# Two attention branches in one Trainium2 program: half tiles for A's values, a second query tile turned by TensorE, and a new order of work

## The chip, the cores and the metric

The program runs on one core of a Trainium2 chip. The core has five engines with a queue of instructions each: TensorE (PE in the profile, with its weight loads PEld), VectorE (DVE), ScalarE (ACT), GpSimd (POOL) and SyncE (SP), which here only issues transfers. The metric is the device time of the program in microseconds (us), as the median of several executions.

## The reference

Two independent branches work on 2048 tokens of width 640, with 32 heads of 20 channels, and their outputs stand side by side. The core of each, cut:

```python
# A: four segments of 512 tokens, causal attention inside a segment, and a memory over the earlier ones
p = _softmax(einsum('bhqd,bhkd->bhqk', qs, ks) * scale + mask)
a_dot = einsum('bhqk,bhkd->bhqd', p, vs)
a_mem = einsum('bhld,bhde->bhle', phi(qs), M) / (einsum('bhld,bhd->bhl', phi(qs), z)[..., None] + 1e-06)
o = g * a_mem + (1.0 - g) * a_dot
M = M + einsum('bhld,bhle->bhde', phi(ks), vs); z = z + einsum('bhld->bhd', phi(ks))
...
return o @ wo
# B: causal attention with a sliding window of 256 tokens
scores = where(mask, einsum('bhqd,bhkd->bhqk', q, k) * Dh ** (-0.5), -1e9)
o = einsum('bhqk,bhkd->bhqd', _softmax(scores), v)
return o.reshape(B, S, D) @ wo
```

## The kernel before

The work is cut into eight chunks of 512 tokens, A and B in turn: A0, B0, A1, B1, A2, B2, A3, B3 (numbers 0 to 7). A chunk needs its projections (q, k, v), its scores, the exponentials, the masks, the product with the values, the division, the memory (A only) and the output projection.

**Scores and values.** `score_batch` (line 801) issues one batch: matmuls of 20 channels for four heads at a time, on four row strips of the array, into two PSUM tiles named `sc`, and behind them two exponentials on ScalarE (line 830) that write probability tiles `pt`. There are 153 batches and three `sc` tiles, so a batch's second tile waits until the exponential of the batch before has read it. GpSimd zeroes triangles of `pt` (line 869), VectorE multiplies others with a mask (line 847). `av` (line 883) and, in the last chunk, `av_tile` (line 904) multiply `pt` with the values, on four column strips. VectorE turns the result in 32x32 blocks (line 949), takes reciprocals (line 977), and GpSimd multiplies into `o` (line 987).

**Projections.** `wide` (line 935, or line 930 on four column strips) issues the matmuls of 512 or 320 columns for q, k, v and the output, into one of two PSUM banks, `m0` and `m1`, from which VectorE copies them (lines 557, 733, 738, 1100). A bank is free again when that copy is done.

**Values of A.** `vA` is one tile of 128 x 4 x 696 for all 32 heads. `v_job` writes it in two jobs, heads 0 to 15 and 16 to 31 (line 733). After each job two transfers copy half of its rows into `vS` (line 757), from where the products with the squares on the diagonal read. The program waits by tile: an instruction that reads one half of `vA` can wait for a write to the other half.

**The end.** A query tile of the last chunk (128 tokens) needs `o` with its channels on the partitions. For tiles 0, 1 and 2 `final` stores `o` to a buffer in memory (line 1021, four transfers), and a transposing transfer brings it back (line 1040); `final_job` then multiplies with the output weights. The last tile is turned on TensorE in `last_job`: four matmuls with a unit matrix (line 1122) and sixteen small ones (line 1134) put `o` into PSUM, VectorE and ScalarE copy it (lines 1126 and 1140) into free corners of `pq` and `pkT`, ten matmuls with re-ordered output weights follow in two halves (`last_half`), ScalarE copies the one (line 1157) and VectorE the other (line 1160), and two transfers store them (line 1164).

**The order.** No scheduler runs at run time. `PLAN` lists every step of TensorE: `S` or `s` is a score batch, `A` the product with the values for the next group of heads, `M` a product with the memory, `k20*5` five matmuls of the k projection of chunk 2, `o71*4` four of the output projection of chunk 7's tile 1, `d4` the memory's update, `z0` a step of `last_job`. Where an `A` follows a capital `S`, the projections beside it run on column strips. The instructions of the other engines are placed as a model of their times in `Flow` says when TensorE gets there; at run time each engine takes its queue in that order.

Of the kernel before, what the change touches and what calls it, by code (L numbers as in the profile page):

```python
# [60 lines left out]
PLAN = (  # L61
# [22 lines left out]

# [183 lines left out]
class _K:  # L268
# [391 lines left out]
    def dm_job(self, seg, pkT, v):  # L660
# [12 lines left out]
        for some in (own, [(lambda kt, h=h: spare[:, kt, R2 * h:R2 * h + R2], R2,  # L673
# [6 lines left out]
            for lhs, rows, xs, g0 in some:  # L680

                gs = [g0] if g0 is not None else sorted(MEM2[x][1] for x in xs)
                n = W * len(gs)
                v0 = at_head(4 * gs[0])
                for kt in range(LT):
                    nc.tensor.matmul(dM[0:rows, at:at + n], lhsT=lhs(kt),  # L686
                                     rhs=v[:, kt, v0:v0 + n],
                                     start=(kt == 0), stop=(kt == LT - 1))
                f.on_pe("full", 4 * mm_ns(n), 4 * n, 0.0, 4)
                at += n  # L690
                if (rows, xs) != (some[-1][1], some[-1][2]):
                    yield 0.0
# [22 lines left out]
    def v_job(self, n, half, w_ap, v, gate, needs):  # L715
# [5 lines left out]
        for tt in range(LT):  # L721
            yield "bank"
            ps, bi = self.bank()
            for kt in range(self.KT):
# [4 lines left out]
            src = ps[:, 0:320].rearrange("p (h e) -> p h e", e=DH)  # L729
            dst = v[:, tt, HV * half:HV * half + 16 * VS].rearrange(  # L730
                "p (h e) -> p h e", e=VS)[:, :, 0:DH]
# [15 lines left out]
    def v_squares(self, n, half, v):  # L747


        f = self.f  # L750
        s = slice(HV * half, HV * half + HV)
        tok = v[0:SH, :, s].rearrange("p (a b) c -> p a b c", b=2)
        t = f.dve + 138.0

        def go():
            for odd in (0, 1):
                self.nc.sync.dma_start(
                    out=self.vS[SH * odd:SH * odd + SH, odd * 2:odd * 2 + 2, s],
                    in_=tok[:, :, odd, :])
                tl = f.on_dma(1, 410.0, t) + (1200.0 if n == 0 else 0.0)  # L760
            for g in range(4 * half, 4 * half + 4):
                self.mark(tl, n, "v", g)
        f.at(t, go)

    def v_ends(self, n, c, half, v):
# [15 lines left out]
        def go():  # L781
# [3 lines left out]
            for g in range(4 * half, 4 * half + 4):  # L785
                self.mark(tl, n, "v", g)
        f.at(t, go)

    def v_tile(self, name, now=True):
# [84 lines left out]
    def av(self, parts, g, vof):  # L874
# [4 lines left out]
        for n_, (ref, q0, nq, c0, pts) in enumerate(parts):  # L879
            v = vof(ref)  # L880
            for j in range(4):
                h = 4 * g + j
                nc.tensor.matmul(O[HD * j:HD * j + HD, q0:q0 + nq],  # L883
                                 lhsT=v[:, at_head(h):at_head(h) + HD],
                                 rhs=pts[j // 2][:, j % 2, c0:c0 + nq],
# [162 lines left out]
    def final_job(self, n, wo, out2d, r0, col, t0, t1, there):  # L1048
# [4 lines left out]
        for tt in range(t0, t1):  # L1053
            if n == len(self.chunks) - 1 and tt == LT - 2:

                row = r0 + tt * P
                for hf in range(2):
                    yield "bank"
                    self.last_half(hf, lambda m: oT[:, m, tt * P:(tt + 1) * P], wo,
                                   out2d[row:row + P], col)  # L1060
                continue
            while self.ring("ot", NOT) is None:
# [45 lines left out]

    def last_job(self, o, wo, out2d, r0, col, t):


        nc, f = self.nc, self.f
        yield t
        yield self.sc_free[-NSC]
        two = self.ps.tile([P, 2, 512], F32, name="sc", bufs=NSC)
        self.sc_free.append(f.pe + 3000.0)
        own = len(self.sc_free) - 1
        b0 = LT * (LT - 1)
        wide = two[:, 0, :].rearrange("p (j b t) -> p b j t", j=4, b=LT)
        one = self.one[:].rearrange("p (j t) -> p j t", j=4)  # L1120
        for b in range(LT):
            nc.tensor.matmul(wide[:, b], lhsT=o[:, b0 + b, 0:P], rhs=one, start=True, stop=True,
                             skip_group_check=True)
            f.on_pe("full", mm_ns(P), P)
        oT = [self.pq[:, 0, 0:4 * P], self.pkT[:, 0, 0:P]]
        nc.vector.tensor_copy(out=oT[0], in_=two[:, 0, :])
# [16 lines left out]
        oT = [oT[m // 4][:, P * (m % 4):][:, 0:P] for m in range(self.KT)]  # L1143
        row = r0 + (LT - 1) * P
        for hf in range(2):
# [158 lines left out]
    def body(self, xA, A_wq, A_wk, A_wv, A_wo, A_beta, xB, B_wqkv, B_wo, out2d):  # L1304
# [41 lines left out]
        self.vX = big.tile([P, VW], BF16, name="vX")  # L1346
        self.vA = self.v_tile("vA")
        self.vS = big.tile([P, LT, VW], BF16, name="vS")
        self.consts_mz()
# [7 lines left out]
        self.consts_ends()  # L1357
        nc.gpsimd.memset(self.vS[:].bitcast(F32), 0.0)
        f.on_pool(10500.0)
# [208 lines left out]
    def one_group(self, n, kind, c, g, what, parts, left, o_t, groups_done, scro, wo, out2d):  # L1568
# [3 lines left out]
        def vof(ref):  # L1572
            what, u = ref
            if what == "a":
                return self.vA[:, u, :]
            if what in "st":
                return self.vS[:, 2 * (u % 2) + u // 2, :]
            if what == "l":
# [12 lines left out]
        if what == "tile":  # L1591
# [11 lines left out]
            def last(t):  # L1603
                if g0 == G - 4:
                    if qt == LT - 1:
                        self.fins.insert(0, self.job(self.last_job(o, wo["end"], out2d, c * L, col, t), "z0"))
                        return
# [105 lines left out]
```

## Time and profile before

| | us |
|---|---|
| median of three runs | 330.22 |
| lowest and highest | 328.9, 330.69 |
| the profiled execution's own time | 329.68 |
| its span, first to last instruction | 328.0 |
| TensorE busy | 315.8 (96%) |
| ScalarE busy | 299.5 (91%) |
| GpSimd busy | 265.3 (81%) |
| VectorE busy | 255.6 (78%) |

A matmul's busy time overlaps the next one's, so 96% says that TensorE rarely stood idle, not that it worked at its peak. The granted clock of TensorE was 1.00 in all stretches from 0 to 328 us. The views used are the page, the busy time by stretches, the waits (who waited for whom), the chain that ended last, the timeline, and the view of one source line. "Idle before" is the time that an engine had nothing to do before an instruction, and what ended it. What only a comparison of the two built programs shows, the order of instructions on each engine, is not in a profile; such counts are named as counts of the order.

### The profile page before, as it was taken

The page shows a single profiled execution, that of the slowest core. Times are in us where ns is not written, and L with a number is a line of the kernel's source. Part 1 is how long each engine was busy: PE and PEld are TensorE (multiplying, and loading weights), DVE is VectorE, ACT ScalarE, POOL GpSimd, SP SyncE. Part 2 cuts the span into 40 slices and gives each one's busy share as a digit, 9 for nine tenths or more (in the row PEclk, how much of TensorE's full clock was granted, in tenths as well). Part 3 has the DMA queues.
Part 4 walks back from the last instruction along what each step waited for, and adds up shares of the span by engine and source line. Part 5 has one row for each costly group of instructions (what it writes and reads, how often), then busy time and mean ns, then how long its engine had stood idle before and what let it go on. Part 6 is the DMA issues. An engine that isn't in the chain of part 4 may idle for free. (4 is left out here: it accounts for less than half of the span.)

```text
span 328.0 us, 16968 instructions
## 1 busy us (share of the span) xinstructions
PE 315.8 (96%) x7195; PEld 176.3 (54%) x7195; DVE 255.6 (78%) x533; ACT 299.5 (91%) x333; POOL 265.3 (81%) x672
## 2 busy tenths in 40 slices
PE   8999999999999999999999999999999999999995
PEld 2454546555544455555654545456655445666663
DVE  6777767789877887998877897988776788876763
ACT  2979999999999998989999999899999999979982
POOL 8466689998769899977885999998976899998761
PEclk9999999999999999999999999999999999999999
DMA  7975845773689566164689146116968126587752
GB/s 207 400 253 124 199 142 90 162 199 64 137 222 182 108 161 180 38 138 145 142 218 170 28 87 156 52 26 133 156 184 194 26 48 157 141 203 186 119 122 88
DMA packets 76266, 47.45 MB, mean 145 GB/s; under 512 B 48382, under 2 KB 73182, under 8 KB 76190
## 3 DMA queue, kind: packets, MB, share of 16 engines
q1 hardware_dynamic: 75469, 45.71, 58.5%
q8 instruction: 56, 0.92, 1.2%
q10 hardware_dynamic: 720, 0.66, 0.7%
q14 instruction: 21, 0.16, 0.2%
HBM read 17.62 MB, written 16.96 MB: 105 GB/s over the span
## 5 line engine op out<-in xcount | busy, mean ns | idle before, releaser
L830 ACT ACTIVATE pt<-sc 128x1024 bf16<-128x1024 f32 (+2 forms) x306 | 282.5, 1024 | 14.4 <-PE sc L814 12.4
L869 POOL TENSOR_SCALAR_AFFINE_SELECT pt<-pt 128x128 bf16<-128x128 bf16 (+1 forms) x512 | 178.0, 376 | 48.9 <-ACT pt L830 42.0
L949 DVE STREAM_TRANSPOSE tt<-m 128x512 f32<-128x512 f32 x88 | 61.2, 709 | 24.9 <-PE m L883 16.1
L987 POOL TENSOR_TENSOR o<-tt,rr 128x320 bf16<-128x320 f32 x64 | 48.4, 757 | 3.6 <-DVE rr L977 2.6
L814 PE MATMUL sc<-qB,kB 20*64 20x64 bf16 (+2 forms) x1728 | 39.6, 217 | 1.0 <-ACT pt L830 0.3
L935 PEld LDWEIGHTS <-xT 128*128 128x128 bf16 x296 | 26.7, 97 | 18.3 <-issue 6.5
L847 DVE TENSOR_TENSOR pt<-pt,ends 128x1024 bf16<-128x1024 bf16 (+2 forms) x50 | 36.3, 737 | 0.0
L1100 DVE CAST ot<-m 128x320 bf16<-128x320 f32 x58 | 28.1, 486 | 9.4 <-PE m L935 8.2
L814 PEld LDWEIGHTS <-kB 20*64 20x64 bf16 (+1 forms) x1728 | 22.0, 98 | 22.5 <-issue 20.7
L814 PE MATMUL sc<-qA,kA 20*64 20x64 bf16 (+4 forms) x1024 | 33.4, 237 | 0.3 <-ACT pt L830 0.3
L935 PEld LDWEIGHTS <-oT 128*128 128x128 bf16 x244 | 21.4, 97 | 11.9 <-issue 2.6
L814 PEld LDWEIGHTS <-kA 20*128 20x128 bf16 (+1 forms) x1024 | 13.5, 97 | 22.2 <-issue 21.1
L935 PE MATMUL m<-wBv,xT 128*128 128x320 bf16 x147 | 24.2, 299 | 0.9 <-DVE tt L949 0.4
L883 PE MATMUL m<-pt,vA 128*32 128x192 bf16 (+3 forms) x512 | 23.6, 274 | 0.2
L935 PE MATMUL m<-xT,wBq 128*128 128x512 bf16 x82 | 21.4, 380 | 0.3 <-DVE tt L949 0.3
L935 PE MATMUL m<-wo_A,oT 128*128 128x320 bf16 x125 | 21.0, 301 | 0.3 <-DVE kA L557 0.3
L935 PE MATMUL m<-xT,wBk 128*128 128x512 bf16 x81 | 20.7, 381 | 0.0
L935 PE MATMUL m<-wv_A,xT 128*128 128x320 bf16 x119 | 19.8, 300 | 0.7 <-issue 0.5
L738 DVE CAST vB<-m 128x320 bf16<-128x320 f32 x32 | 15.6, 489 | 5.3 <-PE m L935 3.1
L935 PE MATMUL m<-wo_B,oT 128*128 128x320 bf16 x109 | 18.6, 300 | 0.6 <-DVE tt L949 0.4
L557 DVE CAST qB<-m 128x512 bf16<-128x512 f32 x20 | 13.8, 688 | 6.7 <-PE m L935 3.4
L557 DVE CAST kB<-m 128x512 bf16<-128x512 f32 x20 | 13.6, 681 | 6.6 <-PE m L935 5.6
(127 smaller groups left out, 464.1 us busy)
## 6 DMA issues: line engine op xcount, KB each, us to landing
out_dram<-ot SPq DMA_DIRECT2D x29, 160.0 KB
scr_o<-o SPq DMA_DIRECT2D x28, 160.0 KB
xT<-in_B_x_dram SPq DMA_DIRECT2D x8, 288.0 KB
xT<-in_A_x_dram SPq DMA_DIRECT2D x8, 256.0 KB
scr_pk<-e SPq DMA_DIRECT2D x15, 128.0 KB
vS<-vA SPq DMA_DIRECT2D x16, 87.0 KB
vL<-vB SPq DMA_DIRECT2D x8, 174.0 KB
scr_kA<-kA SPq DMA_DIRECT2D x16, 60.0 KB
```

Of the source, the lines that this page charges most:

```text
L557: nc.vector.tensor_copy(out=dst[:, m, at:at + L], in_=ps[:, :])
L738: nc.vector.tensor_copy(out=dst, in_=src)
L814: nc.tensor.matmul(ps[j // 2][h0:h1, j % 2, c0:c0 + nq], lhsT=k[rows, g, k0:k0 + h1 - h0], rhs=q[rows, g, q0:q0 + nq], start=True, stop=Tr ...
L830: nc.scalar.activation(out=pt[:, :, lo:hi], in_=ps[i][:, :, lo:hi], func=ACT.Exp, scale=self.scale)
L847: nc.vector.tensor_tensor(out=blk, in0=blk, in1=self.ends[:, c0, :].unsqueeze(1).unsqueeze(1) .to_broadcast([P, 2, n // SH, SH]), op=ALU.mult)
L869: nc.gpsimd.affine_select(out=blk, in_=blk, pattern=pat, compare_op=ALU.is_ge, fill=self.zero, base=base, channel_multiplier=mul)
L883: nc.tensor.matmul(O[HD * j:HD * j + HD, q0:q0 + nq], lhsT=v[:, at_head(h):at_head(h) + HD], rhs=pts[j // 2][:, j % 2, c0:c0 + nq], start= ...
L935: self.nc.tensor.matmul(ps[:, 0:n], lhsT=lhsT, rhs=rhs, start=start, stop=stop, skip_group_check=True)
L949: self.nc.vector.transpose(out=tt[:], in_=O[:, :])
L987: nc.gpsimd.tensor_tensor(out=to[:] if add_to else to, in0=a, in1=b, op=ALU.mult)
L1100: nc.vector.tensor_copy(out=ot[:, 320 * hf:320 * hf + 320], in_=ps[:, 0:320])
```

## The change

Three things. `vA` and `vS` become two tiles each, one for 16 heads. The third query tile of the last chunk (tile 2) goes through `last_job` instead of memory; its steps are `z0`, the last tile's are now `z1`, and they may begin only when all scores are issued. `PLAN` is a new list; the counts of its steps differ in these `o72` and `z` steps alone.

```diff
-    "k00*5 q00*5 k01*4 S k01 q01*5 S v00*16 S v00*4 k02 S k02*4 k03*5 q02*3 S q02*2 q03*5 k04*5 "
+    "q00*5 k00*5 k01*5 s q01*5 v00*4 S v00*14 s v00*2 q02*3 S q02*2 q03*5 k02*3 S k02*2 k03*5 "
...
-    "s o40*5 o50*3 s o50*2 o40*5 o50*2 s o50*3 A s o50*10 s A o50*2 s o50*9 s o50*9 s A o60*5 s "
-    "o60*5 o70*5 A o70 s o70*4 o60*5 s o60*5 o71*4 s o71*6 o60*2 s o60*6 A o60*8 A o60*4 o72*2 "
-    "z0*4 ")
+    "o50*9 s A o50*2 s o50*8 s o50*8 s A o60*5 s o60*10 o70 s o70*4 A s o60*5 o70*5 s o60*5 "
+    "o71*4 s o71 A z0 o71*5 o60*10 A z0 o60*5 z0 z1*2 z0 z1*2 ")
...
-                v0 = at_head(4 * gs[0])
+                v0 = at_head(4 * gs[0]) - HV * (gs[0] // 4)
-                                     rhs=v[:, kt, v0:v0 + n],
+                                     rhs=v[gs[0] // 4][:, kt, v0:v0 + n],
...
-            dst = v[:, tt, HV * half:HV * half + 16 * VS].rearrange(
+            own, c0 = (v[half], 0) if gate else (v, HV * half)
+            dst = own[:, tt, c0:c0 + 16 * VS].rearrange(
...
-                    out=self.vS[SH * odd:SH * odd + SH, odd * 2:odd * 2 + 2, s],
+                    out=self.vS[half][SH * odd:SH * odd + SH, odd * 2:odd * 2 + 2, :],
...
+    def half_tiles(self, name):
+        return [self.big.tile([P, LT, HV], BF16, name="%s%d" % (name, x)) for x in range(2)]
...
-            if n == len(self.chunks) - 1 and tt == LT - 2:
-                row = r0 + tt * P
-                for hf in range(2):
-                    yield "bank"
-                    self.last_half(hf, lambda m: oT[:, m, tt * P:(tt + 1) * P], wo,
-                                   out2d[row:row + P], col)
-                continue
...
-    def last_job(self, o, wo, out2d, r0, col, t):
+    def last_job(self, o, wo, out2d, r0, col, t, qt):
-        yield self.sc_free[-NSC]
+        yield lambda: self.sc_free[-NSC] if self.all_scored else None
-        b0 = LT * (LT - 1)
+        b0 = LT * qt
+        own_x = LT - 1 - qt
-        oT = [self.pq[:, 0, 0:4 * P], self.pkT[:, 0, 0:P]]
+        oT = [self.pq[:, own_x, 0:4 * P], self.pkT[:, own_x, 0:P]]
...
-                    if qt == LT - 1:
-                        self.fins.insert(0, self.job(self.last_job(o, wo["end"], out2d, c * L, col, t), "z0"))
+                    if qt >= LT - 2:
+                        self.fins.insert(0, self.job(self.last_job(
+                            o, wo["end"], out2d, c * L, col, t, qt), "z%d" % (qt - LT + 2)))
                         return
```

In the order of the built programs TensorE has 7195 matmuls before and 7218 after; the 23 more are a second set of 4 + 16 turning matmuls and three from where a projection runs whole or on column strips. It changes between the four forms (whole array, row strips of 32 and of 64 columns, column strips) 338 times before and 336 times after. Of VectorE's 32 writes to A's values, the program lists a transfer among what they wait for in 13 before and in 5 after. Ahead of the same batch of scores TensorE has, in whole projection matmuls, five of 512 columns more before the 28th batch and six more before the 61st, four of 512 fewer before the 99th, and three of 320 fewer before the last, the 153rd; before the 150th it has one product with the values (64 matmuls on column strips) fewer, which comes right behind that batch.

More of the change, by code (lines that the diff above doesn't have):

```diff
@@ L750, in v_squares @@
         f = self.f
-        s = slice(HV * half, HV * half + HV)
-        tok = v[0:SH, :, s].rearrange("p (a b) c -> p a b c", b=2)
+        tok = v[half][0:SH].rearrange("p (a b) c -> p a b c", b=2)
         t = f.dve + 138.0
@@ L881, in av @@
             for j in range(4):
-                h = 4 * g + j
+                at = at_head(4 * g + j) - (HV * (g // 4) if ref[0] in "ast" else 0)
                 nc.tensor.matmul(O[HD * j:HD * j + HD, q0:q0 + nq],
-                                 lhsT=v[:, at_head(h):at_head(h) + HD],
+                                 lhsT=v[:, at:at + HD],
                                  rhs=pts[j // 2][:, j % 2, c0:c0 + nq],
@@ L1143, in last_job @@
         oT = [oT[m // 4][:, P * (m % 4):][:, 0:P] for m in range(self.KT)]
-        row = r0 + (LT - 1) * P
+        row = r0 + qt * P
         for hf in range(2):
@@ L1346, in body @@
         self.vX = big.tile([P, VW], BF16, name="vX")
-        self.vA = self.v_tile("vA")
-        self.vS = big.tile([P, LT, VW], BF16, name="vS")
+        self.vA = self.half_tiles("vA")
+        for t in self.vA:
+            nc.gpsimd.memset(t[:, :, 0:16 * VS].rearrange("p t (h e) -> p t h e", e=VS)[
+                :, :, :, DH], 1.0)
+            nc.gpsimd.memset(t[:, :, HV - 12:HV], 1.0)
+        self.vS = self.half_tiles("vS")
         self.consts_mz()
@@ L1357, in body @@
         self.consts_ends()
-        nc.gpsimd.memset(self.vS[:].bitcast(F32), 0.0)
+        for t in self.vS:
+            nc.gpsimd.memset(t[:].bitcast(F32), 0.0)
         f.on_pool(10500.0)
@@ L1574, in vof @@
             if what == "a":
-                return self.vA[:, u, :]
+                return self.vA[g // 4][:, u, :]
             if what in "st":
-                return self.vS[:, 2 * (u % 2) + u // 2, :]
+                return self.vS[g // 4][:, 2 * (u % 2) + u // 2, :]
             if what == "l":
```

37 rows, old and new, of the table PLAN are left out of this document.

## The prediction

> **What bounds the kernel now.** I read the page first, then the busy time by stretches, then the waits. The page gives the span and says that TensorE and ScalarE both work nearly all the time:
>
> ```profile
> span 328.0 us, 16968 instructions
> ...
> PE 315.8 (96%) x7195; PEld 176.3 (54%) x7195; DVE 255.6 (78%) x533; ACT 299.5 (91%) x333; POOL 265.3 (81%) x672
> ...
> PE 33%; ACT 5%; DVE 4%; DMA 2%; issue 2%; POOL 2%; SPq 0%; ACTq 0%; DVEq 0%
> ```
>
> The last line, the chain that ended last, is mostly TensorE; transfers have 2% of it. The stretches (length, then busy time and instructions of PE, PEld, DVE, ACT, POOL, then the granted clock) say where which of the two leads:
>
> ```profile
> 41.00:123.00 82.00, 79.75 (x1771) 43.08 (x1769) 65.61 (x140) 80.27 (x92) 70.31 (x183) 1.00 0.66 147
> 123.00:164.00 41.00, 39.12 (x1019) 23.81 (x1016) 35.76 (x75) 37.88 (x42) 34.57 (x73) 1.00 0.53 129
> 164.00:205.00 41.00, 40.20 (x881) 21.07 (x880) 32.83 (x69) 40.28 (x44) 34.69 (x96) 1.00 0.58 132
> 205.00:246.00 41.00, 40.52 (x1057) 24.11 (x1045) 34.04 (x69) 38.34 (x42) 36.45 (x79) 1.00 0.50 110
> 246.00:287.00 41.00, 40.30 (x880) 20.93 (x879) 32.78 (x71) 40.59 (x45) 35.60 (x97) 1.00 0.49 113
> 287.00:319.00 32.00, 31.37 (x906) 20.62 (x899) 21.73 (x45) 28.45 (x31) 25.62 (x63) 1.00 0.75 158
> ```
>
> From 41 to 123, 164 to 205 and 246 to 287 us ScalarE is idle for 1.7, 0.7 and 0.4 us: there it is full, and moving TensorE's work can win almost nothing. From 123 to 164, 205 to 246 and 287 to 319 it is idle for 3.1, 2.7 and 3.6 us while TensorE is for 1.9, 0.5 and 0.6: there TensorE's work and its waits set the pace. ScalarE's idle time is about what a new order can win at most, and by the waits (total, times, longest) it is nearly all for scores; the second row is what the half tiles aim at:
>
> ```profile
> ACT pt L830 <- PE sc L814: 12.4, 23, 2.0
> ...
> PEld L883 <- DVE vA L733: 0.7, 2, 0.5
> ```
>
> **The half tiles.** They take away waits between one half of A's values and the other. The view of line 733, VectorE's writes to `vA`, lists what ended its idle time; three rows of the timeline follow:
>
> ```profile
> its engine sat idle before it (us, times) until:
>   PE m L935: 0.8, 4
>   PE m L930: 0.6, 2
> ...
> 28.09 0.40 PE L814 MATMUL sc<-qA,kA 20*128 20x320 bf16 x8
> 28.53 0.48 DVE L733 TENSOR_TENSOR vA<-m,omg 128x320 bf16<-128x320 f32 x1
> ...
> 29.06 0.31 PEld L883 LDWEIGHTS <-vA 128*32 128x32 bf16 x12 [0.53 <-DVE vA L733]
> ```
>
> No transfer is in that list: the program's waits on the `vS` transfers had been met before VectorE came to them, so taking eight of those away is worth nothing here. What covers it is VectorE's own queue; were the transfers late by more than that, the writes and the banks behind them would wait. The wait at 29.06 us is a real one: by the order the product reads the first half (`vA0` after), and the write that ends at 29.01 is to the second. TensorE's scores ended at 28.49, and with a change of form (0.1 us, sized below) and the load it could go on at about 28.85: it loses 0.2 us. The bounds are 0 and the 0.7 of the waits; I take -0.2.
>
> On GpSimd the tiles cost three more fills at the start. It stood idle for 1.91 us ahead of its first mask, at 9.85, behind the last fill, so they are covered: zero. Were they longer than that, the first masks would be late, and the products behind them.
>
> ```profile
> 9.85 0.54 POOL L869 TENSOR_SCALAR_AFFINE_SELECT pt<-pt 128x128 bf16<-128x128 bf16 x2 [1.91 <-ACT pt L830]
> ```
>
> **The head.** The q projection now goes first, and all five matmuls of `k01` stand ahead of the first batch instead of four:
>
> ```profile
> 6.17 1.24 PE L935 MATMUL m<-xT,wq_A 128*128 128x512 bf16 x5
> ...
> 8.32 0.40 PE L814 MATMUL sc<-qA,kA 20*128 20x448 bf16 x8
> ...
> 8.76 1.02 ACT L830 ACTIVATE pt<-sc 128x1024 bf16<-128x1024 f32 x1 [0.24 <-PE sc L814]
> ```
>
> Five matmuls of 512 columns take 1.24 us, the last of them 0.38 to its end, so one costs (1.24 - 0.38) / 4 = 0.22 us. Before, the batch waited some 0.1 us for the copy of q, and with q first that copy is done earlier. So +0.1 us, between 0 and +0.2.
>
> **The end.** These rows of the timeline carry the sum:
>
> ```profile
> 300.92 0.45 PE L935 MATMUL m<-wo_B,oT 128*128 128x320 bf16 x2
> ...
> 301.30 1.02 PE L814 MATMUL sc<-qB,kB 20*64 20x64 bf16 x64
> ...
> 313.52 0.72 PE L935 MATMUL m<-wo_B,xT 128*128 128x320 bf16 x4 [0.26 <-DMA xT<-scr_o]
> ...
> 315.76 0.40 PE L814 MATMUL sc<-qB,kB 20*128 20x128 bf16 x16
> 315.78 3.54 POOL L869 TENSOR_SCALAR_AFFINE_SELECT pt<-pt 128x256 bf16<-128x256 bf16 x8 [2.35 <-ACT pt L830]
> ...
> 319.25 0.30 PE L904 MATMUL m<-pt,vB 128*32 128x128 bf16 x8
> ...
> 320.60 1.52 PE L935 MATMUL m<-wo_B,xT 128*128 128x320 bf16 x10
> ...
> 322.11 0.40 PE L1122 MATMUL sc<-one,o 128*128 128x128 bf16 x4
> 322.44 0.30 PE L1134 MATMUL sc<-one,o 128*32 128x32 bf16 x16
> 322.57 0.68 DVE L1126 CAST pq<-sc 128x512 bf16<-128x512 f32 x1
> ...
> 323.31 0.72 PE L935 MATMUL m<-wk_A,pq 128*128 128x320 bf16 x4 [0.56 <-DVE pq L1126]
> ```
>
> A 320-column matmul costs (1.52 - 0.30) / 9 = 0.136 us, with 0.30 for the last one to its end as in the row at 319.25. A change of form costs 301.30 - 300.92 - 2 x 0.136 = 0.1 us.
>
> Up to the last batch of scores TensorE has three such matmuls fewer (-0.41) and two form changes fewer (-0.2), and the 0.26 for tile 1's transfer goes, because its first matmul now stands a batch later: the batch comes 0.87 us earlier, if ScalarE keeps up. It can: from 287 us on it has 3.6 us of holes.
>
> Behind that batch, before, there are 14 matmuls of 320 and one product until the last product, 319.25 - 315.76 = 3.5 us. After, there are 16 matmuls, the product and tile 2's four turning matmuls (322.44 - 322.11 less a form change, 0.23): 3.5 + 0.27 + 0.23 = 4.0. The masks of the last product ended 315.78 + 3.54 = 319.32, 3.56 behind the batch, so they are now covered. From the last product to tile 3's turn VectorE and GpSimd set the time, 322.11 - 319.25 = 2.9 us; TensorE has the product, ten matmuls of 320 and tile 2's sixteen small ones there, some 2.5 us, and still waits. In the 0.56 that it waited for the copy at 323.31 it now does tile 2's second half, 5 x 0.136 = 0.68 and the output copies with it: +0.15. Together 0.5 + 0.15 - 0.87 = -0.2. Of what moves: tile 2's copy of 0.68 on VectorE stands ahead of two output copies and the last reciprocal, which have slack as long as the last product is not done; four stores and a transposing load leave SP's queue, ahead of which two output stores waited. The bounds: +0.65 if ScalarE keeps the batch where it was, -0.6 if the turning falls into waits.
>
> A rule of the Trainium skill speaks against the turn: TensorEngine Tiling (Array Packing), Key Properties, has the array drain whenever the tiling mode changes. The 0.1 us above agrees. With four drains for the added set the end would come out at +0.2 instead; in the order its pieces stand beside work of their own form.
>
> For the turn speaks VectorE: DVE Perf Modes, The three transpose paths, of the Trainium skill: 390 ns on TensorE and 1309 ns by a transfer for a block of 128x128. Five blocks would save some 4.6 us, an estimate from that page; here that is time of a transfer under which TensorE worked, and the 0.26 is all that showed.
>
> **The order elsewhere.** Whether ScalarE starves decides what a moved block costs:
>
> ```profile
> 60.93 1.72 ACT L830 ACTIVATE pt<-sc 128x1024 bf16<-128x1024 f32 x2
> ...
> 61.20 0.34 PE L814 MATMUL sc<-qB,kB 20*128 20x256 bf16 x8
> ...
> 126.78 1.94 ACT L830 ACTIVATE pt<-sc 128x1024 bf16<-128x1024 f32 x2
> ...
> 127.18 0.40 PE L814 MATMUL sc<-qB,kB 20*128 20x256 bf16 x12
> ...
> 130.29 1.02 ACT L830 ACTIVATE pt<-sc 128x1024 bf16<-128x1024 f32 x1 [0.66 <-PE sc L814]
> ...
> 208.80 1.02 ACT L830 ACTIVATE pt<-sc 128x1024 bf16<-128x1024 f32 x1 [1.26 <-PE sc L814]
> ...
> 310.63 1.02 ACT L830 ACTIVATE pt<-sc 128x1024 bf16<-128x1024 f32 x1 [0.80 <-PE sc L814]
> ```
>
> The 28th batch (61.20) and the 61st (127.18) come behind five and six more 512-column matmuls: 1.1 and 1.3 us later. Their exponentials, the second of each pair, followed the ones before without a hole, and by the rows the scores had been there for only 0.3 and 0.1 us. So holes of 0.8 and 1.2 us open. Against that the 99th (208.80) comes four such matmuls, 0.9 us, earlier, into a hole of 1.26. TensorE's sum changes at none of the three, and where it leads they cost and win nothing. I take 0; both ends are rivals.
>
> **The sum.** -0.2 (half tiles) + 0.1 (head) - 0.2 (end) + 0 (elsewhere) = -0.3 us, so 329.4 for an execution like the profiled one, of 329.68 us, whose span leaves 1.7 us around it. It lies 0.5 below the median of 330.22; for the median the forecast is 329.9. Its own range, from the bounds, is 328.9 to 331.1. A measurement here can tell 0.5%, 1.65 us, from no change.
>
> **Rivals.** *The order fills ScalarE's holes (faster).* The 0.9 at the 99th batch and the 0.80 at the 150th (310.63; its product with the values now stands behind it) are kept to the end, and half of the 1.9 us that TensorE waits from 123 to 164 goes: -0.9 - 0.8 - 0.95 = -2.6, so 327.6. For it: where ScalarE is idle, those two holes are among the longest. Against it: TensorE's work in these stretches is the same in sum.
>
> *ScalarE starves at the moved blocks (slower).* Its new holes of 0.8 and 1.2 us at the 28th and 61st batch are not made up, for from 41 to 123 us it is full: +2.0, so 332.2. It decides if the holes that follow, 0.66 at 130.29 first, stay as long as they were. Against it: each later hole takes up some of it.
>
> *The half tiles do nothing (same).* The wait at 29.06 is replaced by the next, for the bank or a mask: 330.1.
>
> *The turn lands on the last path (same).* Tile 2's work delays the end and no batch comes earlier: -0.1 + 0.65, so 330.8.
>
> **How the numbers follow.** The forecast with the two rivals that end beside it: 0.44; holes filled: 0.29; starved: 0.27. The range goes 0.2 and 0.4 beyond the values of the outer two, so that about 1 in 10 is left out on each side: 327.4 to 332.6. Faster by over 0.5% (below 328.6) 0.29, within 0.44, slower (above 331.9) 0.27.
>
> **What would show it.** Right: at the tenth batch no wait of a `vA` product for line 733; no hole ahead of tile 1's first matmul; the last batch 0.9 us earlier and the last product 4.0 behind it; holes at the 28th and 61st batch that are made up within ten us. Wrong: ScalarE's idle time between its first and last exponential, or TensorE's waits from 123 to 246 us, changed by over 1.5 us; a wait for `o` or for a copy of over 0.6 us in the end.

## The result, and the profile after

| | before | after |
|---|---|---|
| median, lowest and highest (us) | 329.79 (328.90 to 330.69, 6 runs) | 334.99 (332.26 to 338.08, 6 runs) |
| ratio, 95% interval | | 1.0126 (1.0078 to 1.0174) |
| profiled execution, its span | 329.68, 328.0 | 334.04, 332.3 |

The changed kernel is slower by 1.3%. (All ratios leave out the executions that ran over 1.5% above the fastest of the same kernel, which medians and ranges keep; two of the experiments' executions, of 477.50 and 477.10 us at a mean granted clock of 0.56, are of that kind.) The forecast was 329.9, and the median lies 2.4 us above the upper end of its range. The page of the changed kernel, with two rows of the span in 40 slices of 8.3 us and the row of the granted clock:

```profile
span 332.3 us, 16967 instructions
PE 316.6 (95%) x7181; PEld 177.9 (54%) x7218; DVE 256.5 (77%) x534; ACT 299.9 (90%) x334; POOL 265.0 (80%) x674
PE   8999999999999699999999999999999999999995
ACT  2989999899999759899999999899999999979972
PEclk9999999999999969999999999999999999999999
PE 63%; DVE 9%; ACT 8%; POOL 7%; issue 7%; DMA 4%; SPq 1%; POOLq 0%; ACTq 0%; DVEq 0%
```

The work is the same to within 1 us on TensorE and 0.4 on ScalarE, and the span is 4.3 us longer. TensorE has one slice at 6, the one from 108 to 116 us; in the next one the clock is at 6 and ScalarE at 5. The chain that ended last runs far more over other engines than before (TensorE 63% of it, transfers 4%). (The page lists 7181 of 7218 matmuls; some 0.2 us gaps called "issue" are probably missing records.) By stretches the loss is in the one from 41 to 123 us, where ScalarE was busy 80.27 of 82 us before:

```profile
41.00:123.00 82.00, 76.13 (x1651) 40.35 (x1666) 61.55 (x129) 74.89 (x86) 64.62 (x169) 0.96 0.58 133
```

The waits of the whole span (total, times, longest) name it. The first of them was 12.4 in 23 before, the other two were not there:

```profile
ACT pt L834 <- PE sc L818: 16.3, 20, 3.3
...
DVE vB L739 <- DMA vU<-vB: 4.6, 2, 3.7
...
PE m L887 <- DVE vB L739: 3.0, 1, 3.0
```

VectorE's write of B's values waited 3.7 us at one place for a transfer that reads those values, and TensorE waited 3.0 us behind it. (The other of its two waits, 0.84 us at 196.58, is small beside it.) The chain of the changed kernel around that place, and VectorE's row with its wait:

```profile
112.62 2.55 DMA vU<-vB
...
115.83 1.26 PE m L887 x32
```

```profile
115.29 0.49 DVE L739 CAST vB<-m 128x320 bf16<-128x320 f32 x1 [3.73 <-DMA vU<-vB]
```

The write is the first of `v31`, the second half of the heads of B1 (chunk 3). It fills columns that the transfer does not touch: `v_ends` (line 783) copies rows of the first half to `vU`, `vX` and `vL`. But `vB` is still one tile for both halves, and the program waits by tile. Behind the write one of the two banks stays taken, and A1's product with the values (line 887), which needs a bank, stands at the head of TensorE's queue.

Why the transfer is late shows in SyncE's own queue, first before, then after (start, length, how many):

```profile
97.20 4.61 SPq L646 DMA_TRANSPOSE pkT<-scr_pk  x1
101.98 2.92 SPq L1040 DMA_TRANSPOSE oT<-scr_o  x1
104.95 0.58 SPq L783 DMA_DIRECT2D vU<-vB  x1
...
108.12 0.61 SPq L783 DMA_DIRECT2D vX<-vB  x1
```

```profile
96.43 3.21 SPq L1025 DMA_DIRECT2D scr_o<-o  x4
99.68 1.56 SPq L355 DMA_DIRECT2D xT<-in_A_x_dram  x2
103.72 3.16 SPq L1044 DMA_TRANSPOSE oT<-scr_o  x1
106.92 2.86 SPq L646 DMA_TRANSPOSE pkT<-scr_pk  x1
109.83 0.59 SPq L783 DMA_DIRECT2D vU<-vB  x1
...
113.28 0.60 SPq L783 DMA_DIRECT2D vX<-vB  x1
```

The new order puts chunk 1's `oT` transpose ahead of A1's `pkT`. It must wait for the stores it reads back, and from 101.24 to 103.72 us SyncE issues nothing, with `pkT` and the five value transfers queued behind it. SyncE's list of waits from 93 to 116 us:

```profile
SPq L1044 <- DMA scr_o<-o: 2.3, 1, 2.3
```

The Trainium skill has a sentence for it (DMA: Bandwidth & Descriptors, Anatomy of one DMA, a section on transfers that GpSimd issues): a wait on a semaphore is spent on the engine that issues, before the transfer is handed over. This row agrees.

So two margins moved at once. Before, the last of the five transfers was issued at 108.12 and the write came at 115.28, 7.2 us later. After, the last was issued at 113.28 and VectorE was ready at 115.29 - 3.73 = 111.56, 1.7 us *earlier*: the transfers are 5.2 us later and the write 3.7 earlier, since `v31` now starts two batches sooner in `PLAN`. The place of `oT` in the queue accounts for about 3 of the 5.2 us (3.3 and 2.9 in two experiments below). The stores of `o` and two loads of x, which also stand later in the queue than before, come ahead of it; their share was not measured apart.

The stop has a second price. TensorE's rows around it, and one stretch of the busy times with the granted clock in the third column from the end:

```profile
112.25 0.61 PE L934 MATMUL m<-xT,wBq 128*32 128x512 bf16 x8
115.83 0.99 PE L887 MATMUL m<-pt,vA 128*32 128x448 bf16 x12 [2.97 <-DVE vB L739]
...
117.57 0.61 PE L939 MATMUL m<-xT,wBk 128*128 128x512 bf16 x1
...
118.83 1.49 PE L939 MATMUL m<-xT,wBk 128*128 128x512 bf16 x3 [0.22 <-issue]
...
121.05 0.61 PE L818 MATMUL sc<-qA,kA 20*128 20x320 bf16 x8
...
114.78:121.61 6.83, 5.56 (x60) 2.26 (x64) 4.36 (x9) 1.94 (x2) 3.88 (x11) 0.50 0.24 39
```

A matmul of 512 columns takes (1.49 - 0.61) / 2 = 0.44 us there, twice the 0.22 of before. The granted clock is at half from 114.78 to 121.61 us: it fell 1.9 us after TensorE's last matmul (112.25 + 0.61 = 112.86), before the stop was over.

### The profile page after: what moved, and what is told of

It reads as the page before. It is cut to its first block, busy times and chain, and to the rows that moved or that the text cites. A ratio compares the mean times of both kernels' runs of the same rounds, so it can differ in the third digit from the quotient of the medians.

```text
span 332.3 us, 16967 instructions
## 1 busy us (share of the span) xinstructions
PE 316.6 (95%) x7181; PEld 177.9 (54%) x7218; DVE 256.5 (77%) x534; ACT 299.9 (90%) x334; POOL 265.0 (80%) x674
## 4 chain that ended last, share of the span: by engine, by line
PE 63%; DVE 9%; ACT 8%; POOL 7%; issue 7%; DMA 4%; SPq 1%; POOLq 0%; ACTq 0%; DVEq 0%
PE m L939 30%; PE sc L818 12%; PE m L887 9%; PE m L934 9%; ACT pt L834 7%; POOL pt L873 5%; DVE tt L953 4%; DMA vU<-vB 2%; POOL o L991 1%; PE m L686 1%; DMA wq_A<-in_A_wq_dram 1%; DVE pt L851 1%; ACT e L577 1%; POOL u L991 1%; DMA scr_qA<-qA 1%
## 5 line engine op out<-in xcount | busy, mean ns | idle before, releaser
L834 ACT ACTIVATE pt<-sc 128x1024 bf16<-128x1024 f32 (+2 forms) x306 | 283.1, 1020 | 17.8 <-PE sc L818 16.3
L818 PE MATMUL sc<-qB,kB 20*64 20x64 bf16 (+2 forms) x1728 | 41.0, 217 | 1.4 <-issue 0.4
L851 DVE TENSOR_TENSOR pt<-pt,ends 128x1024 bf16<-128x1024 bf16 (+2 forms) x50 | 37.2, 755 | 0.0
L818 PE MATMUL sc<-qA,kA 20*64 20x64 bf16 (+4 forms) x1024 | 34.1, 239 | 0.3
L939 PE MATMUL m<-wv_A,xT 128*128 128x320 bf16 x130 | 22.0, 300 | 0.2 <-DVE rr L981 0.2
L939 PE MATMUL m<-wo_A,oT 128*128 128x320 bf16 x131 | 21.9, 300 | 0.2 <-DVE tt L953 0.2
L939 PE MATMUL m<-xT,wq_A 128*128 128x512 bf16 x77 | 20.9, 384 | 0.9 <-DMA wq_A<-in_A_wq_dram 0.5
L991 POOL TENSOR_TENSOR u<-tt,rr 128x320 bf16<-128x320 f32 x24 | 18.2, 758 | 3.7 <-DVE rr L978 3.4
L939 PE MATMUL m<-xT,wBq 128*128 128x512 bf16 x67 | 18.4, 380 | 1.1 <-DVE tt L953 0.6
L887 PEld LDWEIGHTS <-vA 128*32 128x32 bf16 x512 | 12.3, 97 | 13.1 <-DVE vB L739 3.9
```

The costliest lines, as they stand in the source:

```text
L818: nc.tensor.matmul(ps[j // 2][h0:h1, j % 2, c0:c0 + nq], lhsT=k[rows, g, k0:k0 + h1 - h0], rhs=q[rows, g, q0:q0 + nq], start=True, stop=Tr ...
L834: nc.scalar.activation(out=pt[:, :, lo:hi], in_=ps[i][:, :, lo:hi], func=ACT.Exp, scale=self.scale)
L851: nc.vector.tensor_tensor(out=blk, in0=blk, in1=self.ends[:, c0, :].unsqueeze(1).unsqueeze(1) .to_broadcast([P, 2, n // SH, SH]), op=ALU.mult)
L887: nc.tensor.matmul(O[HD * j:HD * j + HD, q0:q0 + nq], lhsT=v[:, at:at + HD], rhs=pts[j // 2][:, j % 2, c0:c0 + nq], start=(n_ == 0), stop= ...
L939: self.nc.tensor.matmul(ps[:, 0:n], lhsT=lhsT, rhs=rhs, start=start, stop=stop, skip_group_check=True)
L991: nc.gpsimd.tensor_tensor(out=to[:] if add_to else to, in0=a, in1=b, op=ALU.mult)
```

## The experiments

All shifts below are of one kind: the start of a batch's first score matmul, less the same in the profile of before, in us, with the shift of the span's end in the last column. Each row is one profiled execution; the rows "again" are the second profiles of two kernels.

```
batch          9th  29th  53rd  54th  56th  61st  68th  77th 117th 149th 153rd | span
after        -0.23 +0.63 -0.02 +3.66 +5.71 +7.19 +5.54 +4.84 +4.79 +4.81 +3.97 | +4.3
after again  -0.41 +0.09 -0.43 +4.51 +6.02 +7.48 +5.85 +5.30 +5.11 +6.69 +5.85 | +6.2
oT later     +0.23 +1.62 +1.07 +2.26 +2.85 +4.31 +2.71 +2.05 +1.70 +1.99 +1.15 | +1.5
vB halves    -0.27 +0.66 +0.02 +0.02 +0.46 +1.92 +0.32 -0.38 -0.74 -0.23 -1.07 | -0.7
vB again     -0.04 +0.84 +0.29 +0.29 +0.73 +2.19 +0.55 -0.15 +0.65 +0.91 +0.66 | +1.0
v31 later    +0.08 +0.54 +0.10 +0.28 +1.40 +2.66 +1.50 +1.23 +0.88 +0.91 +0.07 | +0.4
order back   +0.03 +0.03 +0.04 +0.04 +0.04 +0.04 +0.06 -0.22 -0.06 -0.06 -0.91 | -0.1
half tiles   +0.23 +0.23 -0.21 -0.21 -0.21 -0.20 -0.19 -0.48 -0.38 -0.38 -0.76 | -0.7
both repairs -0.08 +0.37 -0.05 -0.05 +0.39 +1.85 +0.22 -0.48 -1.14 +1.19 +0.35 | +0.7
```

**The transpose of `oT` behind the values' transfers.**

```diff
-            f.blocked.append((tl - 200.0, room, lambda t_: turn(tl)))
+            f.blocked.append((tl - 200.0, late if n == 1 else room, lambda t_: turn(tl)))
...
+        def late():
+            return self.done.get(("pkT", 1))
```

> The changed kernel with one transfer moved in SyncE's queue: the transpose of chunk 1's outputs (oT) is issued behind that of A1's key features (pkT) and the six small transfers of values that follow it, instead of ahead of them. Theory (queue): the 3.7 us for which VectorE's first write of chunk 3's second half of values (L739) waits for the transfer vU<-vB is due to that order. The transfers go out 5 to 7 us earlier, the write waits under 0.5 us, TensorE's stop of 3.1 us ahead of the product of the 55th batch is gone, the granted clock in 82:123 is 1.00 again, and the batches from the 55th on start 5 to 6 us earlier: 328.3 to 330.0 us. Rival (ScalarE starves where blocks were moved, at the 29th and 61st batch): nothing changes, 333 to 336 us. Rival (the turn of the third query tile in the tail costs it): also 333 to 336 us.

Measured: 331.03 us (329.41 to 335.11, 10 runs), ratio 1.0034 (1.0007 to 1.0062); clock 1.00 from 82 to 123 us. The rows of this kernel, SyncE's queue and the write:

```profile
103.24 3.52 SPq L646 DMA_TRANSPOSE pkT<-scr_pk  x1
106.81 0.59 SPq L783 DMA_DIRECT2D vU<-vB  x1
...
110.62 3.70 SPq L1047 DMA_TRANSPOSE oT<-scr_o  x1
...
114.23 0.49 DVE L739 CAST vB<-m 128x320 bf16<-128x320 f32 x1 [1.59 <-DMA vU<-vB]
...
114.78 0.59 PE L887 MATMUL m<-pt,vA 128*32 128x448 bf16 x12 [0.83 <-DVE vB L739]
```

About three quarters of the loss are gone (0.34% left of 1.26%, in two comparisons) with one transfer moved and nothing else changed, so the order of SyncE's queue is a cause. The rest was expected to go as well, and did not: the median lies above the expected 330.0, the transfers went out 3.3 us earlier (113.28 against 109.98) and not 5 to 7, and the wait is still 1.59 us, because `vU<-vB`, issued at 109.32, took 4.79 us to land by the chain of this run, against 2.55 above.

**B's values in half tiles, the queue left as it is.**

```diff
-            own, c0 = (v[half], 0) if gate else (v, HV * half)
+            own, c0 = v[half], 0
...
-            todo += [(self.vU[hi, 0:2, :], pv[hi, 2:4, :], 820.0),
-                     (self.vX[lo, :], pv[lo, 0, :], 410.0)]
+            for x in range(2):
+                z = slice(HV * x, HV * x + HV)
+                todo += [(self.vU[hi, 0:2, z], pv[x][hi, 2:4, :], 410.0),
+                         (self.vX[lo, z], pv[x][lo, 0, :], 205.0)]
...
-        self.vB = [self.v_tile("vB0"), self.v_tile("vB1")]
+        self.vB = [self.half_tiles("vB0"), self.half_tiles("vB1")]
```

> The changed kernel with B's values, too, in a tile for each half; the queue keeps its order, and six small transfers become twelve halves of them over the kernel. Theory (queue and the shared tile): the write of the second half waited only because the transfers that read the first half read the same tile. With tiles of their own the write waits for nothing, though the transfers still go out as late as at 109 to 114 us: 328.5 to 330.2 us. If instead the late transfers themselves are what is needed (their readers, the products of chunk 3), the stop moves to those products a few batches on and the time stays above 332 us. Rivals (ScalarE at the moved blocks, or the tail): 333 to 336 us.

Measured: 330.01 us (327.80 to 333.25, 10 runs), ratio 1.0008 (0.9969 to 1.0047). The write goes out at once:

```profile
111.51 0.49 DVE L739 CAST vB<-m 128x320 bf16<-128x320 f32 x1
```

The first value transfer is issued at 109.87 us in this run and the last at 114.19, no earlier than in the changed kernel, and no reader of them waits. So nothing needed the transfers early: the wait was one for the tile alone. From the 56th batch to the 91st the changed kernel stands 5.2 us behind this one throughout (5.3 in the second profiles of both, from the 56th to the 68th), which is the price of the wait. Behind the second, small wait at 196.58 the distance goes to 5.8 and settles at 5.5. Half of these ten runs came out at 331 to 333 us with a mean clock of 0.99, so the kernel was run once more:

> The changed kernel with B's values in half tiles, once more, for its scatter: half of its runs were at 328 to 329 us with a clock of 1.00 and half at 331 to 333 with 0.99. If a run of the second kind is profiled, the page shows where TensorE stops for over 2 us, and it is not at v31's first write, which waits for no transfer now; a guess is a later transfer of the values or of pkT that lands too late for its reader. Median 328.5 to 331.5 us.

Measured: 328.49 us (327.83 to 331.85, 10 runs), ratio 0.9965 (0.9934 to 0.9996), clock 1.00 in the profile, so no run of the other kind was seen in detail, and what stops TensorE in them stays open. The kernel before shows the same in the later comparisons, in five of 58 at 332.7 to 333.9 us with a mean clock of 0.994 or 0.995, so B's half tiles need not be its cause.

**`v31` two batches later.**

```diff
-    "... q33*3 s v31*5 q33*3 S q33*2 A s k33 M k33*4 v31*3 S v31*2 A M ..."
+    "... q33*3 s q33*5 k33 S k33*2 A s k33 M k33 v31*8 S v31*2 A M ..."
```

> The changed kernel with one stretch of its order rewritten: the eight matmul steps of chunk 3's second half of values (v31) start two batches later, and the q and k steps between them come first. The queue keeps its order there. Theory: the first write of v31 comes some 4 us later, when the transfer it waits for has landed or lands within 1 us; the stop goes from 3.1 us to under 1, the clock stays up, 328.5 to 331 us (what the keys of the stretch being earlier or later does is not known better than 1 us). Rivals that need no wait of L739: 333 to 336 us.

Measured: 332.43 us (330.06 to 333.73 in nine runs, and one of 477.50), ratio 1.0074 (1.0042 to 1.0105); its profiled execution took 330.15. The first write of `v31` comes at 116.65 us and waits for no transfer, and the clock stays at 1.00. The wait is gone, as expected, but the median is above what was expected: the table has this kernel 0.7 to 1.6 us behind the one with B's half tiles from the 56th batch on, which may be the price of the rewritten stretch itself; that was not shown apart, and no cause was traced for the scatter of its runs.

**The new order of the queue, put into the kernel before.**

```diff
+        def behind():
+            return gate() if 1 in self.oT else None
...
-                    f.blocked.append((tl + 5000.0, gate, lambda t0: turn(max(t0, tl))))
+                    f.blocked.append((tl + 5000.0, behind if c == 1 else gate,
+                                      lambda t0: turn(max(t0, tl))))
```

> The kernel before with the changed kernel's order in SyncE's queue at one place: chunk 1's oT transpose ahead of A1's pkT and the values' transfers. Theory (the order of the queue hurts only together with the earlier start of v31): the transfers go out 2 to 3 us later than the 104.95 to 108.74 us of before, but the first write of v31 comes at 114.9 us, after they have landed: its wait stays under 0.5 us and the time within 0.5% of before, 329 to 331 us. If the order alone were enough, the write would wait over 2 us and the time be above 332 us.

Measured: 329.98 us (10 runs), ratio 0.9971 (0.9936 to 1.0005). Its rows:

```profile
101.24 2.66 SPq L1044 DMA_TRANSPOSE oT<-scr_o  x1
103.94 3.56 SPq L649 DMA_TRANSPOSE pkT<-scr_pk  x1
...
111.02 0.61 SPq L787 DMA_DIRECT2D vX<-vB  x1
...
114.91 0.43 DVE L742 CAST vB<-m 128x320 bf16<-128x320 f32 x1
```

The transfers are 2.9 us later than before (111.02 against 108.12), and the write at 114.91 does not wait. The order of the queue hurts only together with the earlier `v31`.

**Half tiles of A alone; and the whole change with the order of before.** The first is the kernel before with `vA` and `vS` in halves. The second is the changed kernel with the order of before up to the tail and its own tail (from `o60*5 s o60*10 o70 s` on).

> The kernel before with A's values in half tiles and nothing else: its own order, its own end. By the prediction's first term the wait of the tenth batch's product goes and little else changes: minus 0.2 us, 329 to 330.2 us. Rival (the half tiles themselves cost the 5 us, through the queue or through the ones written at the start): above 332 us.

> The changed kernel with the order of before up to the tail (the first 148 batches' moves undone) and its own tail: half tiles and both turned query tiles stay. Theory: what is lost is in the order around the 55th batch alone; with it gone the rest of the change shows what the prediction gave it, minus 0.2 for the half tiles and minus 0.2 (0.9 earlier last batch, less 0.65 of added tail work and wait) for the end: 328.7 to 330.2 us, granted clock 1.00. Rival (the turn in the tail costs): above 331 us.

Measured: half tiles alone 330.35 us, ratio 0.9994 (0.9958 to 1.0031); order of before 330.61 us, ratio 0.9990 (0.9947 to 1.0032), each with 10 runs, beside 35 runs of before at 330.06 in the same comparison. Both medians lie a little above what was expected. Neither can be told from no change, neither shows the 5 us, and the write of B's values does not wait in either. So the 5 us came with the new order before the tail. The wait at the tenth batch, which half tiles alone were expected to take away, is still there:

```profile
28.32 0.40 PE L817 MATMUL sc<-qA,kA 20*128 20x320 bf16 x8
...
28.76 0.48 DVE L733 TENSOR_TENSOR vA<-m,omg 128x320 bf16<-128x320 f32 x1
...
29.29 0.31 PEld L886 LDWEIGHTS <-vA 128*32 128x32 bf16 x12 [0.53 <-DVE vA L733]
```

**The price of the clock.** Fourteen matmuls on constants fill TensorE's stop; they go into a score tile that nothing reads, and nothing else moves.

```diff
                         pend.pop(0)
+                        if (n, g) == (2, 4):
+                            two = self.ps.tile([P, 2, 512], F32, name="sc", bufs=NSC)
...
+                            for _ in range(14):
+                                self.nc.tensor.matmul(two[:, 0, :], lhsT=c1, rhs=c5, start=True, stop=True)
```

> The changed kernel with 14 matmuls of 128x512 on constants put ahead of the product of the 55th batch's stage that waits (chunk 2, fifth group), into a score tile that nothing reads: about 3.0 us of TensorE work at 213 ns each, in the time in which it stands still. Nothing else moves. Theory: the write still waits some 3 to 3.7 us for the transfer, but TensorE has no stop of over 1 us and so keeps its clock; the matmuls behind it go at 213 ns and not at 427, and 2 to 2.5 us of the 5.7 lost at this place come back: 331.5 to 332.7 us. Rival (the clock drop has another cause, or costs nothing since ScalarE sets the pace): 333.5 to 336 us, with 427 ns matmuls behind the wait as before, or without them and no faster.

Measured: 333.92 us (333.71 to 335.09, 4 runs), ratio 1.0130 (1.0089 to 1.0172), above what was expected. The clock stayed at 1.00, but in the profiled execution the transfer took 3.51 us to land and the write waited 4.78, against 2.55 and 3.73, which took the gain away. So the two kernels, the changed one and the one with the constant matmuls, were run side by side:

> The changed kernel itself, unaltered, beside the other three on one chip, since the earlier runs of it and of its variants were not on the same one. Theory: the wait of v31's first write is 2.5 to 5 us, set by how late the transfer lands in that run, the granted clock falls behind it, and the time is 332.5 to 337 us.

> The changed kernel with the 14 constant matmuls ahead of the product that waits, once more, with the unaltered changed kernel beside it. In the first run of it the transfer vU<-vB took 3.5 us to land instead of 2.6 and the wait was 4.8 us instead of 3.7, so the times could not be told apart. Theory (clock): counted from the moment the write of v31 begins, the 57th batch starts 1.5 to 2.2 us sooner than in the unaltered kernel, and the median is 1 to 2.5 us below its median. Rival (the clock costs nothing beyond the wait): same distance from the write to the 57th batch within 0.4 us, and the same median within 0.7 us.

Measured: the changed kernel 336.72 us (334.32 to 338.72, 4 runs), ratio 1.0181 (1.0116 to 1.0247); with the constant matmuls 334.95 (333.81 to 335.80, 4 runs), ratio 1.0119 (1.0055 to 1.0183). The intervals overlap, so the 1.8 us between the medians rest on few runs; the rows are clearer. First the changed kernel in this comparison, then the one with the constant matmuls:

```profile
116.68 0.99 PE L887 MATMUL m<-pt,vA 128*32 128x448 bf16 x12 [4.23 <-DVE vB L739]
...
119.25 1.91 PE L939 MATMUL m<-xT,wBk 128*128 128x512 bf16 x4
...
121.57 0.40 PE L818 MATMUL sc<-qA,kA 20*128 20x320 bf16 x8
```

```profile
113.03 3.23 PE L1493 MATMUL sc<-const-bfloat16-1.0 128*128 128x512 bf16 x14
117.39 0.59 PE L887 MATMUL m<-pt,vA 128*32 128x448 bf16 x12 [1.12 <-DVE vB L739]
...
119.52 1.02 PE L939 MATMUL m<-xT,wBk 128*128 128x512 bf16 x4
...
121.00 0.40 PE L818 MATMUL sc<-qA,kA 20*128 20x320 bf16 x8
```

From the product's first matmul to the 55th batch, the second behind it, it is 121.57 - 116.68 = 4.9 us in the one and 121.00 - 117.39 = 3.6 in the other, with the same work between. In the first profile of the changed kernel it is 121.05 - 115.83 = 5.2, and with `oT` moved, where TensorE stood for 0.83 us only, 118.40 - 114.78 = 3.6. So the slow clock costs 1.3 to 1.6 us on top of the stop. That is less than the 2 to 2.5 first expected. Counted as set down before the second run, from the start of the write to the 57th batch, it is 125.22 - 116.13 = 9.1 us and 124.66 - 116.84 = 7.8: 1.3 us sooner, less than the expected 1.5 to 2.2, but well over the 0.4 of the rival.

**Both repairs at once.** That is, B's half tiles and the moved `oT`; and the same with the first slice of `wq_A` loaded ahead of that of `wk_A`.

> The changed kernel with both repairs of the place: B's values in half tiles, and chunk 1's oT transpose behind A1's pkT and the values' transfers (the weights at the start in the changed kernel's order). Theory: no wait at v31; 327.8 to 329.8 us where nothing else stops TensorE, so faster than the kernel before by up to 0.5%. If some runs still come out at 331 to 333 us with a clock of 0.99, half tiles of B open another wait (six more small transfers in SyncE's queue), and this version is no better than the kernel before.

> The changed kernel with B's values in half tiles, the oT transpose of chunk 1 behind A1's pkT and the values' transfers, and at the start the first slice of wq_A loaded ahead of that of wk_A (the new order uses it first). Theory: no wait at v31, and the 0.2 to 0.7 us that the first batch is late come back: 327.3 to 329.5 us, below both kernels. If the runs still scatter by 3 to 4 us with a clock below 1.00 in some, there is a further marginal wait that the order holds, elsewhere than at v31.

Measured: both repairs 328.55 us (327.74 to 331.13, 12 runs), ratio 0.9944 (0.9910 to 0.9978): faster than the kernel before by 0.6% in this one comparison, and no wait at `v31`. With the load swapped 331.55 us (12 runs, 328.18 to 333.68 and one of 477.10), ratio 0.9988 (0.9950 to 1.0027): above what was expected and not faster, and in its profile the first batch came 0.85 us later than before (9.17 against 8.32), so the swap does not bring the head back.

## Why the prediction was wrong

*The step that failed* is "The order elsewhere": "TensorE's sum changes at none of the three, and where it leads they cost and win nothing. I take 0". It counted the matmuls that moved and the holes of ScalarE, and looked at no other queue. The order of SyncE's issues had moved too, and with it the margin between a transfer that reads `vB` and the next write to it, from 7.2 us after the issue to 1.7 before it. Its cost is 5.2 us in place of 0. Beside the kernel with B's half tiles the product starts 3.1 us later (115.83 against 112.73), and from there to the 55th batch it takes 5.2 us against 3.3, of which 1.6 are the slow clock by the comparison above; the other 0.5 is not divided further.

*The half tiles.* The prediction said that the `vS` waits were covered by VectorE's own queue and that, "were the transfers late by more than that, the writes and the banks behind them would wait". That is what happened, with the tile that was not split: the mechanism was in the text, but the margin of `vB` was never read. The term of -0.2 came out in size, but by luck; its mechanism was wrong. At the tenth batch the changed kernel has

```profile
28.10 0.40 PE L818 MATMUL sc<-qA,kA 20*128 20x320 bf16 x8
...
28.20 0.49 DVE L734 TENSOR_TENSOR vA<-m,omg 128x320 bf16<-128x320 f32 x1
...
28.75 0.42 PEld L887 LDWEIGHTS <-vA 128*32 128x32 bf16 x12 [0.21 <-DVE vA L734]
...
28.87 0.58 PE L887 MATMUL m<-pt,vA 128*32 128x448 bf16 x12
```

That is 0.77 us from scores to product, 0.97 before (28.09 to 29.06). But with half tiles alone it is still 0.97 (28.32 to 29.29, the rows above), behind the same write of VectorE, and over the whole span the waits of this kind are 0.7 us in two, as before. So the tile was not what the product waited for. The same write also empties a bank: a q projection that TensorE starts between the scores and the product (28.42 us in the kernel before) has one of the two, the product needs the other, and that is the one which this write reads. This reading follows from the order of the work and was not tested by itself; it is the prediction's rival "The half tiles do nothing", whose next wait is the one for the bank. What the changed kernel gains there comes from its order: VectorE's write starts 0.10 us behind the scores instead of 0.44.

*The head* was +0.23 at the first scores (8.55 against 8.32) and at the first exponential instead of +0.1: q first means waiting for `wq_A`, for which TensorE stood 0.51 us ahead of its first projection, at 4.91 us instead of 4.30; the prediction has no such wait. Its size was off, and it varies: +0.05 to +0.69 at that exponential in the profiles of the kernels that start as the changed one does.

*The end* held in its first part; the size of its second varies. From the 149th batch to the last the changed kernel gains 4.81 - 3.97 = 0.84 us (0.87 forecast). Its rows:

```profile
319.73 0.40 PE L818 MATMUL sc<-qB,kB 20*128 20x128 bf16 x16
...
323.52 0.30 PE L908 MATMUL m<-pt,vB 128*32 128x128 bf16 x8
...
326.38 0.40 PE L1119 MATMUL sc<-one,o 128*128 128x128 bf16 x4 [0.41 <-POOL o L991]
```

The last product stands 3.8 us behind the last batch (4.0 forecast, 3.5 before), and all behind the last batch takes 332.3 - 319.73 = 12.57 us against 328.0 - 315.76 = 12.24: +0.33 instead of +0.65. With the order of before it shows alone: the last batch comes 0.91 earlier, but the span is only 0.1 shorter, so there the part behind the batch costs 0.8. The rival that no batch comes earlier fell, but that the turn wins time at the end was seen in some profiles and not in all.

*The holes* at the 28th and 61st batch opened. In the kernel with B's half tiles, where no wait covers them, the row at the 61st is

```profile
129.62 1.94 ACT L837 ACTIVATE pt<-sc 128x1024 bf16<-128x1024 f32 x2 [1.05 <-PE sc L821]
```

and its shift goes from +0.46 at the 56th batch to +1.92 at the 61st and is back at +0.32 by the 68th, 17 us on, not ten. At the 28th the shift is +1.74, and at the 29th +0.66. So they are made up, and the rival that ScalarE starves there fell, although its 332.2 came nearest to the time: of the changed kernel's 7.19 us at the 61st batch, 7.19 - 1.92 = 5.3 are the wait's. The sign to look for was given as ScalarE's idle time, which did change by over 1.5 us (12.4 to 16.3), but at one place that the prediction had not named.

With the wait taken away, the forecast of -0.3 us stands beside -0.7, +1.0 and +0.7 in the spans of the three profiles (B's half tiles twice, both repairs), and beside ratios of 1.0008, 0.9965 and 0.9944. Whether the rest of the change is worth 0.3 us can't be told from these.

## What to carry to other kernels

When an order of work changes, compare each queue that issues, not only the engines that compute: for every transfer that is moved past another, read when it is issued, when it lands, and when the next instruction that needs it *or that overwrites its source* is ready. A transfer that waits for its own source holds all behind it, so one that nobody needs soon goes behind those that somebody does. Where a tile is split because halves wait for each other, look at every tile that is used in the same way, and ask whether the instruction that the wait names also frees something else, such as a bank; the split alone, run by itself, tells.

## What was not expected of the hardware

A stop of TensorE of 3.0 us was enough for the clock to fall to half for 6.83 us and for 512-column matmuls to take 0.44 us instead of 0.22; stops of 0.8 and 1.1 us were not, nor was the one of 1.94 us below. The clock fell 1.9 us into the stop, in both profiles of the changed kernel. The Trainium skill (TensorE: Matmul & The Clock Gate, HAM oscillation) warns of gaps of more than about 3.4 us; here a shorter one did it.

The same transfer `vU<-vB` took 2.55 to 4.79 us to land in the five profiles in which the write waited for it; the longest was the one with a transposing transfer issued 1.3 us behind it. That the transposing transfer slowed it was not tested.

In the profile of the version with both repairs TensorE stands still inside one batch of scores, and the profile names no engine or transfer for it:

```profile
291.12 0.59 PE L821 MATMUL sc<-qB,kB 20*64 20x64 bf16 x50
293.65 0.26 PE L821 MATMUL sc<-qB,kB 20*64 20x64 bf16 x14 [1.94 <-issue]
```

It is most of the jump from -1.14 to +1.19 in the last row of the table, and there is a like one in the second profile of the changed kernel, of 1.64 us, and in that of the version with the load swapped, of 1.94, but none in the first of the changed kernel. All three come behind the 50th of the 64 matmuls of the same batch, the 141st. In these three a transfer of 16 KB of instructions (queue q8 of the profile) starts within 0.1 us of that batch and lands 0.9 to 1.1 us after its start; in the eleven other profiles of this text it has landed 0.7 to 1.4 us before. So TensorE may have waited for its instructions there; no experiment tested it, and why the transfer comes late in some executions was not found.
